# Moving the K, V and WO loads of a decode kernel from SyncE's hardware queue to GpSimd's software queue

## The chip, the cores and the metric

One core of one Trainium2 chip. The metric is the device time of one execution in microseconds (us). The 25 executions of the kernel before lie between 1273.79 and 1274.54 us. The word "tile" below means one load of K or of V: 128 partitions by 64 KiB, 8.39 MB.

## The reference, cut to what matters

A gated mix of two branches for two tokens. Branch A is one decode step of grouped attention with a cache of 32768 positions, 8 key-value heads, 2 batches; K and V caches together are 537 MB in bf16. Branch B is a small dense layer with a GELU.

```python
g = sigmoid((x * gate_w).sum(-1, keepdims=True))
q = x @ wq                                   # x: 2 x 448, wq: 448 x 4096
p = softmax(q . K * Dh**-0.5)                # K, V: 2 x 8 x 32768 x 256
a = (p . V) @ wo                             # wo: 4096 x 448
b = gelu(x @ w1 + b1) @ w2 + b2              # w1: 448 x 1792, w2: 1792 x 448
out = g * a + (1 - g) * b
```

## The kernel before

The kernel streams K and V through a ring of three slots, each of one tile. All large loads are issued by SyncE, in the order of one list:

```python
order = [("WQ", 0), ("W12", 0)]              # WQ and W12 (w1 and w2) share slot 0
for i in range(NTILES + LAG):                # NTILES = 32, LAG = 2
    if i < NTILES: order.append(("K", i))
    if i >= LAG and i - LAG < LASTV: order.append(("V", i - LAG))
order += [("V", LASTV), ("WO", 0)]
# K0 -> slot 1, K1 -> slot 2, K2 -> slot 0, V0 -> slot 1, K3 -> slot 2, V1 -> slot 0 ...

def released(d):                             # what must have been done before the slot may be refilled
    kind, idx = d
    return {"K": ("S", idx, NCK // 2 - 1), "V": ("PV", idx), "WQ": "QT", "W12": "FB"}[kind]

def prog_sp(E):
    for d in order:
        for pd in before_of[d]:
            E.wait("pe", released(pd))
        # ... e.dma_start(...) for WQ (2 loads), W12 (3), WO (4), the last V (3), every other K or V (1)
```

So K2 cannot be issued before FB, the last matmul that reads W12. TensorE (PE) and VectorE (DVE) work in a fixed order as well:

```python
# PE
do_QT()      # waits for WQ: the query
do_GG()
do_HT()      # waits for W12
do_FB()      # branch B; its end releases slot 0
# ... then scores S(0), S(1), ...; each waits for DVE's transposes of that K tile
# DVE
gelu1(); gelu2()                             # branch B, needs HT
for i in range(LAG): K(i)                    # 8 transposes of 2.27 us for each K tile, in the ring
# ...
```

ACT (ScalarE) issues six very small loads (x, the gate, the biases) on its own hardware queue during the first 3 us.

## Time and profile before

| | before |
|---|---|
| median of 2 runs | 1273.99 us |
| DMA read | 547.4 MB, 430 GB/s over the span |
| DVE busy, PE busy | 54%, 55% |

The page of the kernel before. The row DMA is the mean busy share of the 16 DMA engines in tenths, in 40 slices of the span; under it the GB/s of each slice; then the queue with packets, MB and share of the engines' time.

```profile
span 1272.2 us, 8282 instructions
...
DMA  9999999999999999999999999999999999999998
GB/s 409 429 433 429 437 441 427 433 427 441 431 437 435 429 431 433 439 431 437 435 429 431 439 433 431 439 433 429 431 441 431 435 437 431 431 433 439 431 423 353
...
q1 hardware_dynamic: 10804, 547.43, 99.6%
```

The DMA row shows what bounds the kernel: 9 tenths or more from the first slice to the last but one. DVE and PE are half idle. One data packet here is one row of one partition: 75 loads of 128 rows, and for each load 16 packets of 4 bytes, are 10800 of q1's 10804 packets. A packet of a K tile is therefore 64 KiB, one of WQ 24 KiB.

The start, in lines of the timeline of single engines (start, duration, engine, line of the kernel, operation, output and input, count, and in brackets the idle time before and its releaser; SPq is SyncE issuing a load):

```profile
0.74 0.88 SPq L370 DMA_DIRECT2D ring<-in_A_wq_dram  x2
...
3.54 28.30 SPq L391 DMA_DIRECT2D ring<-in_A_k_cache_dram  x3
...
9.60 0.61 DVE L677 TENSOR_TENSOR gp_sb<-pexp,PT 2x448 f32<-2x448 bf16 x1 [5.52 <-DMA PT<-in_gate_w_dram]
...
12.73 3.55 PE L419 MATMUL ps_s<-xT,ring 128*128 128x2 bf16 x128 [8.24 <-DMA ring<-in_A_wq_dram]
...
20.86 0.34 PE L438 MATMUL ps_m<-xT,ring 128*128 128x2 bf16 x3 [2.63 <-DMA ring<-in_B_w_dram]
...
40.20 17.66 DVE L720 STREAM_TRANSPOSE ring<-ring 128x2048 uint32<-128x2048 uint32 x8 [10.33 <-DMA ring<-in_A_k_cache_dram]
...
59.55 17.66 DVE L720 STREAM_TRANSPOSE ring<-ring 128x2048 uint32<-128x2048 uint32 x8 [1.70 <-DMA ring<-in_A_k_cache_dram]
```

In this trace the queue serves the loads first in, first out. WQ and W12 are used at 12.73 and 20.86 us, K0 is there for DVE at 40.20 and K1 at 59.55, which is 19.35 us later, the time of one tile. The first line of K stands for three issues; the third, K2, was made at 31.5 us, after FB, and lay in the queue for some 26 us: its first packet starts at 57.3. (That is from the packet records of the packed trace: start, length, size and queue of every packet.) The DMA never ran dry. The line of gp_sb: two tiny gate loads on ACT's queue, issued by 1.9 us, were waited for until 9.60.

The same by stretches (from and to, length, the engines' busy time and instructions, granted TensorE clock, DMA share, GB/s; PEld is TensorE's weight load). A packet is counted whole in the stretch in which it starts, so a share can pass 1:

```profile
core 0: us, PE busy (x) PEld busy (x) DVE busy (x) ACT busy (x) POOL busy (x), PEclk, DMA share, GB/s
0.00:180.00 180.00, 106.58 (x798) 30.98 (x518) 105.36 (x88) 9.58 (x36) 3.31 (x14) 0.90 1.00 428
180.00:1180.00 1000.00, 539.64 (x3358) 103.37 (x1306) 549.73 (x403) 32.37 (x143) 0.00 (x0) 0.77 1.00 434
58.00:70.00 12.00, 9.44 (x36) 1.90 (x19) 10.45 (x5) 0.00 (x0) 0.00 (x0) 0.86 1.02 438
130.00:134.00 4.00, 4.00 (x20) 0.86 (x9) 4.00 (x3) 0.00 (x0) 0.00 (x0) 1.00 0.98 426
```

### The profile page before, as it was taken

To read this page: it belongs to the slowest core of one execution; us is meant where nothing else is said; L and a number is where in the kernel's file an instruction comes from. 1 tells how busy PE (TensorE), PEld (TensorE's weight loads), DVE (VectorE), ACT (ScalarE), POOL (GpSimd) and SP (SyncE) were. 2 spreads that over 40 slices of the span, in tenths; PEclk is the share of its full clock that TensorE was granted. 3 is DMA by queue.
4 is the path that set the end of the run, shared out by engine and by line. 5 is a ranking of instruction groups with operands and counts; after the bars stand their busy time and mean duration, and the time that the engine had idled before them with its cause. 6 is when DMAs were issued, how large, how long until landed. Compare 5 with 4: busy or idle time off the path is not lost.

```text
span 1272.2 us, 8282 instructions
## 1 busy us (share of the span) xinstructions
PE 693.5 (55%) x4640; PEld 145.3 (11%) x2112; DVE 686.0 (54%) x529; ACT 43.8 (3%) x184; POOL 3.3 (0%) x14
## 2 busy tenths in 40 slices
PE   4566566545566444765445655445664546654465
PEld 3111111100111000111001111001110001110011
DVE  2675546745376553655635567353665536556351
ACT  1000000000000000000000000000000000000000
POOL 1000000000000000000000000000000000000000
PEclk9978887777887677877778877788877788867786
DMA  9999999999999999999999999999999999999998
GB/s 409 429 433 429 437 441 427 433 427 441 431 437 435 429 431 433 439 431 437 435 429 431 439 433 431 439 433 429 431 441 431 435 437 431 431 433 439 431 423 353
DMA packets 10973, 547.62 MB, mean 430 GB/s; under 512 B 1352, under 2 KB 1616, under 8 KB 1872
## 3 DMA queue, kind: packets, MB, share of 16 engines
q1 hardware_dynamic: 10804, 547.43, 99.6%
q8 instruction: 9, 0.15, 0.0%
q14 instruction: 4, 0.03, 0.0%
q10 hardware_dynamic: 156, 0.01, 0.0%
HBM read 547.43 MB, written 0.00 MB: 430 GB/s over the span
## 4 chain that ended last, share of the span: by engine, by line
DMA 63%; DVE 20%; PE 14%; issue 3%; SPq 0%; another core or an unknown queue 0%; DVEq 0%
DMA ring<-in_A_k_cache_dram 60%; DVE ring L720 18%; PE ps_s L487 4%; PE ps_s L334 4%; PE ps_o L334 3%; DMA ring<-in_A_v_cache_dram 3%; DVE mx L724 1%; PE ps_o L536 1%; PE ps_m L496 0%; PE ps_m L501 0%; DVE gmax L726 0%; PE ps_f L548 0%; DVE gmx L730 0%; SPq L376 0%
## 5 line engine op out<-in xcount | busy, mean ns | idle before, releaser
L720 DVE STREAM_TRANSPOSE ring<-ring 128x2048 uint32<-128x2048 uint32 x256 | 565.2, 2274 | 393.0 <-DMA ring<-in_A_k_cache_dram 392.8
L487 PE MATMUL ps_s<-ring,Abd 128*128 128x512 bf16 x1024 | 426.1, 416 | 429.8 <-DVE ring L720 429.4
L334 PE MATMUL ps_s<-ring,Abd 128*128 128x512 bf16 x1024 | 422.8, 413 | 0.0
L487 PEld LDWEIGHTS ps_s<-ring,Abd 128*128 128x128 bf16 x1024 | 106.0, 104 | 851.5 <-DVE ring L720 483.5
L334 PE MATMUL ps_o<-ring,PT 128*24 128x512 bf16 x1504 | 111.9, 404 | 0.0
L536 PE MATMUL ps_o<-ring,PT 128*24 128x512 bf16 x544 | 57.1, 418 | 12.8 <-DMA ring<-in_A_v_cache_dram 12.8
L506 PE MATMUL ps_f<-o_sb,selg 128*32 128x257 f32 x32 | 17.0, 636 | 83.4 <-DVE o_sb L761 83.4
L761 DVE SCALAR_TENSOR_TENSOR o_sb<-ps_o,mask,o_sb 128x256 f32<-128x256 f32 x112 | 54.2, 484 | 9.1 <-PE ps_o L536 5.1
L724 DVE TENSOR_REDUCE mx<-ps_s 128x1 f32<-128x1024 f32 x16 | 19.6, 1225 | 60.0 <-PE ps_s L334 60.0
L632 ACT ACTIVATE negm<-ps_m 128x1 f32<-128x1 f32 x16 | 2.7, 171 | 1157.6 <-PE ps_m L501 1157.6
L737 DVE STREAM_TRANSPOSE PT<-pexp 128x1024 bf16<-128x1024 bf16 x16 | 19.9, 1244 | 36.8 <-PE ps_o L334 36.8
L536 PEld LDWEIGHTS ps_o<-ring,PT 128*24 128x24 bf16 x544 | 14.6, 98 | 102.3 <-issue 85.3
L734 DVE COPY ls<-lsum 128x1 f32<-128x1 f32 x16 | 2.5, 154 | 31.8 <-ACT pexp L636 31.8
L626 ACT COPY Abd<-qrep 32x16 bf16 (+1 forms) x128 | 19.4, 199 | 0.6
L636 ACT ACTIVATE pexp<-ps_s,negm 128x1024 bf16<-128x1024 f32 x16 | 17.8, 1113 | 1.7
L496 PE MATMUL ps_m<-ident_f,mx 128*1 128x128 f32 x32 | 6.1, 270 | 21.1 <-DVE mx L724 21.1
L758 DVE TENSOR_SCALAR o_sb<-ps_o,mask 128x256 f32<-128x256 f32 x16 | 7.6, 475 | 15.7 <-PE ps_o L334 15.7
L506 PEld LDWEIGHTS ps_f<-o_sb,selg 128*32 128x32 f32 x32 | 2.9, 141 | 101.5 <-DVE o_sb L761 101.5
L501 PE MATMUL ps_m<-ones_f,gmx 1*128 1x1 f32 x32 | 6.0, 256 | 9.9 <-DVE gmx L730 9.9
L726 DVE TENSOR_REDUCE gmax<-ps_m 1x2 f32<-1x128 f32 x16 | 4.5, 278 | 7.5 <-PE ps_m L496 7.5
L419 PE MATMUL ps_s<-xT,ring 128*128 128x2 bf16 x128 | 3.6, 165 | 8.2 <-DMA ring<-in_A_wq_dram 8.2
L501 PEld LDWEIGHTS ps_m<-ones_f,gmx 1*128 1x128 f32 x32 | 4.7, 183 | 14.6 <-DVE gmx L730 14.6
(76 smaller groups left out, 61.5 us busy)
## 6 DMA issues: line engine op xcount, KB each, us to landing
ring<-in_A_v_cache_dram SPq DMA_DIRECT2D x1, 4096.0 KB, 26.8
ring<-in_A_v_cache_dram SPq DMA_DIRECT2D x2, 2048.0 KB, 33.5
ring<-in_A_wq_dram SPq DMA_DIRECT2D x1, 3072.0 KB, 10.6
ring<-in_B_w_dram SPq DMA_DIRECT2D x1, 1568.0 KB, 17.9
ring<-in_A_wo_dram SPq DMA_DIRECT2D x1, 1568.0 KB, 32.4
ring<-in_B_w_dram SPq DMA_DIRECT2D x1, 1344.0 KB, 13.7
ring<-in_A_wo_dram SPq DMA_DIRECT2D x1, 1344.0 KB, 35.3
ring<-in_A_wq_dram SPq DMA_DIRECT2D x1, 512.0 KB, 11.4
```

Of the source, the lines that this page charges most:

```text
L334: return e.add_instruction(mybir.InstMatmult(name=f"I-{nc.next_id()}", engine=mybir.EngineType.PE, ldweights=False, ins=[e.lower_ap(x), e. ...
L487: fn = lambda e, o=o, x=x, st=st, sp=sp, s=s, w=w: e.matmul(o, a_win(s, w), x, start=st, stop=sp, skip_group_check=True)
L501: E.ins(lambda e: e.matmul(ps_m[:, C_BC:C_BC + 1], gmx[:, :], ones_f[0:1, 0:1], start=True, stop=True), key=("M2", g))
L506: E.ins(lambda e: e.matmul(ps_oa, selg[:, :], o_sb[:, :], start=False, stop=False, skip_group_check=True), key=("OT", g))
L536: fn = lambda e, o=o, x=x, wt=wt, st=st, sp=sp, j=j: e.matmul(o, wt, x, start=st, stop=sp, skip_group_check=True)
L626: E.ins(lambda e, o=o, Q=Q, c=c: e.copy(o[:, :, c:c + 2], qrep[32 * Q:32 * Q + 32, :, bass.ds(E.dyn(2 * g, 2), 2)]), key=(("A", g) if (Q = ...
L636: E.ins(lambda e: e.activation(pexp[:, :].rearrange("p (r i a) -> p i r a", r=CR, i=2), ps_s[:, :].rearrange("p (i r a) -> p i r a", i=2, ...
L720: E.ins(lambda e: e.transpose(k_words(idx, blk), k_words(idx, blk)), key=("T", idx, blk))
L724: E.ins(lambda e: e.tensor_reduce(mx[:, :], ps_s[:, :], AX.X, ALU.max), key=("MX", g))
L737: E.ins(lambda e: e.transpose(PT[:, :], pexp[:, :]), key=("PT", g))
L758: E.ins(lambda e, p=p, m=m: e.tensor_scalar(o_sb[:, 0:Dh], p, m, None, op0=ALU.mult), key=("OS0", g))
L761: E.ins(lambda e, p=p, m=m: e.scalar_tensor_tensor(out=o_sb[:, 0:Dh], in0=p, scalar=m, in1=o_sb[:, 0:Dh], op0=ALU.mult, op1=ALU.add), key= ...
```

## The change

K, V and WO are issued by GpSimd; the profile shows them on a queue that it calls software_dynamic, and "software descriptors" below means this path. WQ and W12 stay with SyncE. GpSimd first does its setup (constants), then the loads, in the same relative order. The intent is a test of the other path: it frees SyncE, and nothing else.

```diff
-        def prog_sp(E):
+        def loads(E, kinds):
...
             for d in order:
+                if d[0] not in kinds:
+                    continue
                 for pd in before_of[d]:
                     E.wait("pe", released(pd))
...
+        def prog_pool(E):
+            # ... the setup of constants, as before
+            loads(E, ("K", "V", "WO"))
+
+        def prog_sp(E):
+            loads(E, ("WQ", "W12"))
             E.wait("dve", "mix")
```

(The rest gives WQ a semaphore of its own and swaps two lists of programs.)

More of the change, by code (lines that the diff above doesn't have):

```diff
@@ L196, in bass_gated_mix__gqa_block_cached__dense_activation_gelu__decode_kernel @@
         sch.stream(f"pW{i}", 16)
-    for nm in ("d_w12", "d_x", "d_gw", "d_b", "d_out"):
+    for nm in ("d_wq", "d_w12", "d_x", "d_gw", "d_b", "d_out"):
         sch.stream(nm, 16)
@@ L337, in keep_matmul @@
                 stop_tensor_calc=stop, tile_size=tile[0], tile_position=tile[1], bass_skip_group_check=True))
-        def prog_pool(E):
-            E.ins(lambda e: e.memset(ident_b[:], 0.0), key="ms0")
-            E.ins(lambda e: e.memset(ident_f[:], 0.0), key="ms1")
-            E.ins(lambda e: e.memset(ones_f[:], 1.0), key="ones")
-            E.ins(lambda e: e.memset(xm[:], 0.0), key="xm0")
-            E.wait("pool", "ms0")
-            E.ins(lambda e: e.affine_select(out=ident_b[:], in_=ident_b[:], compare_op=ALU.not_equal, fill=1.0,
-                                          base=0, pattern=[[-1, P]], channel_multiplier=1), key="idb")
-            E.wait("pool", "ms1")
-            E.ins(lambda e: e.affine_select(out=ident_f[:], in_=ident_f[:], compare_op=ALU.not_equal, fill=1.0,
-                                          base=0, pattern=[[-1, P]], channel_multiplier=1), key="idf")
-            E.ins(lambda e: e.memset(Abd[:], 0.0), key="A0")
-            E.ins(lambda e: e.memset(tsel[:], 0.0), key="t0")
-            E.wait("pool", "t0")
-            for b in range(Bn):
-                E.ins(lambda e, b=b: e.affine_select(
-                    out=tsel[:, 136 * b:136 * b + 136], in_=tsel[:, 136 * b:136 * b + 136], compare_op=ALU.not_equal,
-                    fill=1.0, base=256 - 128 * b, pattern=[[-1, 136]], channel_multiplier=-8), key=f"ts{b}")
-        def prog_sp(E):
+        def loads(E, kinds):
             def dma(fn, stream, key):
@@ L369, in prog_sp @@
                     for i, (o, src, _) in enumerate(parts):
-                        dma(lambda e, o=o, src=src: e.dma_start(o, src), "slot0", ("wq", i))
+                        dma(lambda e, o=o, src=src: e.dma_start(o, src), "d_wq", ("wq", i))
                 elif kind == "W12":
@@ L392, in prog_sp, with dma @@
                         f"slot{slot_of[d]}", ("fill", d))
+        def prog_pool(E):
+            E.ins(lambda e: e.memset(ident_b[:], 0.0), key="ms0")
+            E.ins(lambda e: e.memset(ident_f[:], 0.0), key="ms1")
+            E.ins(lambda e: e.memset(ones_f[:], 1.0), key="ones")
+            E.ins(lambda e: e.memset(xm[:], 0.0), key="xm0")
+            E.wait("pool", "ms0")
+            E.ins(lambda e: e.affine_select(out=ident_b[:], in_=ident_b[:], compare_op=ALU.not_equal, fill=1.0,
+                                          base=0, pattern=[[-1, P]], channel_multiplier=1), key="idb")
+            E.wait("pool", "ms1")
+            E.ins(lambda e: e.affine_select(out=ident_f[:], in_=ident_f[:], compare_op=ALU.not_equal, fill=1.0,
+                                          base=0, pattern=[[-1, P]], channel_multiplier=1), key="idf")
+            E.ins(lambda e: e.memset(Abd[:], 0.0), key="A0")
+            E.ins(lambda e: e.memset(tsel[:], 0.0), key="t0")
+            E.wait("pool", "t0")
+            for b in range(Bn):
+                E.ins(lambda e, b=b: e.affine_select(
+                    out=tsel[:, 136 * b:136 * b + 136], in_=tsel[:, 136 * b:136 * b + 136], compare_op=ALU.not_equal,
+                    fill=1.0, base=256 - 128 * b, pattern=[[-1, 136]], channel_multiplier=-8), key=f"ts{b}")
+            loads(E, ("K", "V", "WO"))
+        def prog_sp(E):
+            def dma(fn, stream, key):
+                E.ins(fn, key=key, stream=stream)
+            loads(E, ("WQ", "W12"))
             E.wait("dve", "mix")
@@ L409, in do_QT @@
                 E.wait("act", "xT")
-                E.wait("slot0", ("wq", 1))
+                E.wait("d_wq", ("wq", 1))
                 for h in range(Hq):
@@ L793, in prog_dve @@
                       key=("mix" if q == 1 else None))
-        progs = {"pool": prog_pool, "sp": prog_sp, "pe": prog_pe, "act": prog_act, "dve": prog_dve}
+        progs = {"sp": prog_sp, "pool": prog_pool, "pe": prog_pe, "act": prog_act, "dve": prog_dve}
         engs = {nm: _Eng(sch, nm) for nm in progs}
@@ L807, in run @@
                 progs[nm](engs[nm])
+            block.sync(lambda eng: run("sp", eng))
             block.gpsimd(lambda eng: run("pool", eng))
-            block.sync(lambda eng: run("sp", eng))
             block.tensor(lambda eng: run("pe", eng))
```

## The prediction

> **What bounds the kernel now.** The DMA engines. The page gives 547.42 MB read at a mean of 430 GB/s; the stretch from 100 to 1200 us shows DMA share 1.00 at 433 GB/s. DVE (54%) and PE (55%) wait; 60% of the chain of waits is K loads. A K or V tile is 8.39 MB, 19.4 us at 433 GB/s; V loads land 36.6 us after issue, so even then some 17 us of earlier work are queued. Only an idle gap of the DMA or a lower rate costs time.
>
> **What moves.** 70 loads go from SyncE's queue to GpSimd's; WQ and W12 stay. An issue costs SyncE 0.33 us. [...] With 17 us queued that is hidden. Bytes and rows (64 KiB per partition) stay, so I expect 431-434 GB/s again.
>
> **The step that costs: the start.** Before, one FIFO queue served WQ, W12, K0, K1: WQ was there at 12.7 us (first query matmul), W12 at 20.9, K0 at 40.2, K1 at 59.6, and K2, which waits until WQ and W12 are consumed, was issued at 31.9, long before the queue ran dry. After, K0 and K1 come on another queue from about 4 us (GpSimd's setup ends at 4.02). [...] two tiny gate loads on ACT's queue, issued by 1.9 us, were waited for until 9.6, about one 24 KiB WQ packet (0.9 us) for each of their small ones. A K packet is 64 KiB, 2.4 us. Working the turns through (estimate, 27 KB/us per engine): K0 lands at 29-30 us, WQ at 40-45, K1 at 51, W12 at 57.
>
> FB, the last reader of W12, came 10.3 us after W12: K2 is issued at about 68 and moves from 70: DMA idle from 57 to 70, 13 us. DVE transposes K0 only after the GELU (program order), from 66 to 84 instead of 40 to 58. The ring of three slots then starts with compute behind: V0 issued at 88, K3 at 106, V1 at 133 after K3 has landed at 129: 6 us more of idle DMA. By 160 us the queue is two deep again, but lost time is not won back. Sum: +19 us. The tail changes by 1-2 us at most.
>
> **Prediction.** 1293 us, 8 in 10 between 1279 and 1314. Chances: faster by over 2% 0.01, within 2% 0.70, slower 0.29.
>
> **What would show it.** Right: DMA share near zero at 57-70 us and a dip near 130; WQ consumed after 35 us, W12 after 50; DVE's first transpose of the ring at about 66; K2's issue at about 68; after 160 us 433 GB/s and DVE waiting for K loads as before. Wrong: WQ still at 13 us, or a lower rate between 200 and 1200 us.
>
> **What would make it wrong.** Software descriptors of another size, or a slow engine, that lower the steady rate: each 1% is 12 us. [...] Turns by bytes rather than packets: then WQ and W12 land earlier and the loss shrinks.

+19 us is 13 (57 to 70 us) and 6 (near 130). That the 17 us queued would hide whatever a software load adds was the author's estimate. The turns packet by packet were read from the gate loads of the trace before. In its packet records two packets of 896 bytes, the gate's by their place in the queue, start at 6.42 and 8.28 us, and packets of 4 bytes at 7.37 and 9.23: steps of 0.91 to 0.95 us, where one WQ row takes 0.91. The estimate's 27 KB/us per engine is 433 GB/s over 16 engines.

## The result, and the profile after

| | before | after |
|---|---|---|
| median | 1273.99 us (2 runs) | 1294.80 us (2 runs) |
| ratio, 95% interval | | 1.0163 [1.0138, 1.0187] |

A ratio, here and below, is the mean time of one kernel's fast runs over that of the other's of the same rounds, so not quite the ratio of the medians. The change costs 20.8 us. The page after:

```profile
span 1292.5 us, 8282 instructions
...
DMA  9789899999999999999999999999999999999998
GB/s 402 332 347 430 360 422 440 433 426 446 424 428 446 426 426 446 428 434 436 430 436 432 430 444 426 428 444 428 428 442 430 432 436 432 438 430 430 440 421 357
...
q0 software_dynamic: 9936, 540.55, 96.8%
q1 hardware_dynamic: 724, 6.88, 1.3%
```

The second, third and fifth slices of GB/s (332, 347, 360) are where this row differs; the rest looks as before. The stretches, with the columns of before, tell the same:

```profile
0.00:180.00 180.00, 86.36 (x698) 27.04 (x474) 90.40 (x82) 9.59 (x36) 8.21 (x23) 0.93 0.89 377
180.00:1180.00 1000.00, 546.05 (x3406) 104.48 (x1326) 547.45 (x402) 32.40 (x143) 27.43 (x52) 0.78 1.00 434
58.00:70.00 12.00, 8.75 (x134) 7.64 (x134) 3.31 (x10) 0.23 (x1) 0.00 (x0) 1.00 0.01 2
130.00:134.00 4.00, 3.85 (x19) 0.77 (x8) 1.47 (x2) 0.00 (x0) 0.00 (x0) 1.00 0.06 20
```

From 180 to 1180 us both kernels move 434 GB/s. In the first 180 us the changed one moves 377 GB/s instead of 428; 51 GB/s for 180 us are 9.2 MB, which take 21 us at 433 GB/s. That is the loss, within 0.4 us. Most of it lies in two stretches in which the DMA does next to nothing: 58 to 70 us and 130 to 134 us. (Cut finer, they reach from about 57.4 to 71.7 and from about 129 to 135.8. By the packet records, those of instructions left out, the 16 engines stood idle for a mean of 14.2 us between 57 and 72 us and of 5.0 us between 128 and 136.)

The start in the timeline, as shown for before (POOL is GpSimd):

```profile
0.74 0.87 SPq L353 DMA_DIRECT2D ring<-in_A_wq_dram  x2
...
4.09 1.20 POOL L374 DMA_DIRECT2D ring<-in_A_k_cache_dram  x2
...
41.72 3.55 PE L428 MATMUL ps_s<-xT,ring 128*128 128x2 bf16 x128 [37.20 <-DMA ring<-in_A_wq_dram]
...
59.39 0.34 PE L447 MATMUL ps_m<-xT,ring 128*128 128x2 bf16 x3 [12.17 <-DMA ring<-in_B_w_dram]
...
68.30 35.20 DVE L729 STREAM_TRANSPOSE ring<-ring 128x2048 uint32<-128x2048 uint32 x16
...
70.50 0.53 POOL L374 DMA_DIRECT2D ring<-in_A_k_cache_dram  x1 [65.20 <-PE ps_f L464]
...
133.09 17.66 DVE L729 STREAM_TRANSPOSE ring<-ring 128x2048 uint32<-128x2048 uint32 x8 [2.53 <-DMA ring<-in_A_k_cache_dram]
...
134.56 0.53 POOL L374 DMA_DIRECT2D ring<-in_A_v_cache_dram  x1 [26.54 <-PE ps_s L334]
```

K0 and K1 are issued at 4.09 us, only half a microsecond later than before, but WQ is used at 41.72 instead of 12.73 and W12 at 59.39 instead of 20.86. FB then releases slot 0, and K2 is issued at 70.50, when the queues have been empty for 13 us. DVE begins on K0 at 68.30 although K0 landed 27.2 us after its issue, at 31.3 (K1 landed 49.0 us after its own, at 53.7). From then on compute is behind: V1 waits for the scores of K2 and is issued at 134.56, when K3 has already landed (133.09), and the DMA idles a second time.

In steady state nothing changed: V loads land 36.4 us after issue (36.6 before), K loads 49.5 (49.7). A GpSimd issue took 0.53 us and a SyncE issue 0.33. GpSimd's issues took 527 to 530 ns for all V loads and 527 to 673 for all K loads, though some came while DVE transposed (those at 89.95 and 134.56 us).

### The profile page after: what moved, and what is told of

It reads as the page before. It is cut to its first block, busy times and chain, and to the rows that moved or that the text cites. A ratio compares the mean times of both kernels' runs of the same rounds, so it can differ in the third digit from the quotient of the medians.

```text
span 1292.5 us, 8282 instructions
## 1 busy us (share of the span) xinstructions
PE 691.9 (54%) x4640; PEld 145.0 (11%) x2112; DVE 685.7 (53%) x529; ACT 43.9 (3%) x184; POOL 40.4 (3%) x84
## 4 chain that ended last, share of the span: by engine, by line
DMA 58%; DVE 22%; PE 13%; issue 3%; another core or an unknown queue 3%; ACT 0%; POOL 0%; SPq 0%; DVEq 0%
DMA ring<-in_A_k_cache_dram 52%; DVE ring L729 20%; PE ps_s L496 3%; PE ps_o L334 3%; PE ps_s L334 3%; DMA ring<-in_A_wq_dram 3%; DMA ring<-in_A_v_cache_dram 3%; DVE mx L733 1%; PE ps_o L545 1%; PE ps_m L505 0%; PE ps_m L510 0%; DVE gmax L735 0%; PE ps_m L447 0%; PE ps_s L428 0%
## 5 line engine op out<-in xcount | busy, mean ns | idle before, releaser
L545 PE MATMUL ps_o<-ring,PT 128*24 128x512 bf16 x544 | 57.6, 423 | 12.7 <-DMA ring<-in_A_v_cache_dram 12.7
L374 POOL DMA_DIRECT2D ring<-in_A_v_cache_dram x31 | 16.4, 528 | 960.1 <-PE ps_s L334 957.1
L374 POOL DMA_DIRECT2D ring<-in_A_k_cache_dram x32 | 17.0, 532 | 211.8 <-PE ps_o L334 129.5
L743 DVE COPY ls<-lsum 128x1 f32<-128x1 f32 x16 | 2.5, 154 | 31.8 <-ACT pexp L645 31.8
```

What stands on the lines that cost most here:

```text
L374: dma(lambda e, src=src, d=d: e.dma_start(cut(slot_of[d], 0, SLOT), src), f"slot{slot_of[d]}", ("fill", d))
L545: fn = lambda e, o=o, x=x, wt=wt, st=st, sp=sp, j=j: e.matmul(o, wt, x, start=st, stop=sp, skip_group_check=True)
```

## The experiments

The theory: software descriptors cost nothing that shows; the loss is an accident of order at the start, because two queues with work at the same time take turns here, packet by packet, and the queue with 64 KiB packets gets most of the time (2.42 us for such a packet, 0.91 for a WQ row of 24 KiB). The rivals: software descriptors cost something on each load; turns waste DMA time in themselves; turns go by bytes.

| run | what differs | median us | ratio to before, 95% | WQ, W12 used at | GB/s of the first 180 us |
|---|---|---|---|---|---|
| before | | 1273.95 | | 12.7, 20.9 | 428 |
| after | | 1294.80 | 1.0163 [1.0138, 1.0187] | 41.7, 59.4 | 377 |
| e2 | no software: K0, K1 on ACT's queue | 1293.62 | 1.0154 [1.0137, 1.0170] | 24.7, 59.4 | 382 |
| e3 | one hardware queue, K0, K1 first | 1294.20 | 1.0158 [1.0141, 1.0175] | 50.9, 59.5 | 382 |
| e4 | after, K0 and K1 in 8 KiB rows | 1275.20 | 1.0009 [0.9992, 1.0026] | 16.0, 31.3 | 427 |
| e5 | all loads on GpSimd | 1274.89 | 1.0005 [0.9991, 1.0019] | 13.4, 21.7 | 427 |
| e1 | after, K0 waits for W12 | 1277.82 | 1.0028 [1.0015, 1.0042] | 12.3, 20.7 | 417 |
| e6 | after, only K1 waits for W12 | 1277.66 | 1.0027 [1.0014, 1.0041] | 31.8, 40.2 | 417 |
| e7 | K0, K1 on SyncE, rest on GpSimd | 1292.55 | 1.0144 [1.0127, 1.0161] | 12.4, 21.0 | 382 |
| e8 | e7, K2 waits for K1 | 1278.20 | 1.0034 [1.0018, 1.0051] | as e7 | 417 |

All outputs were correct. Beside e1, e5 and e6 the kernel before had a median of 1274.15 us, beside e8 1273.96. The difference lies in the first 180 us: from 180 to 1180 us every one of them moved 433 or 434 GB/s.

### e2: two hardware queues, no software

```diff
+            E.wait("pool", "ts1")            # GpSimd's setup done, as in the changed kernel
+            loads(E, K0 and K1)              # on ACT, behind its six small loads
...
-            loads(E, ("K", "V", "WO"))       # GpSimd
-            loads(E, ("WQ", "W12"))          # SyncE
+            loads(E, all the others)         # SyncE
```

> No software descriptors at all: K0 and K1 are issued at about 4 us on ACT's hardware queue, everything else on SyncE's. Theory (taking turns between any two queues): WQ used at 39-44 us, W12 at 57-60, K2 issued at 68-72, DMA idle for some 13 us before it and about 5 us near 130, 1290-1298 us. Rival (software descriptors are the cost): 1273-1277 us.

1293.62 us. The loss is there without one software descriptor. Timeline and stretches of this run:

```profile
4.05 0.85 ACTq L374 DMA_DIRECT2D ring<-in_A_k_cache_dram  x2
...
24.68 3.55 PE L429 MATMUL ps_s<-xT,ring 128*128 128x2 bf16 x128 [20.18 <-DMA ring<-in_A_wq_dram]
...
59.44 0.34 PE L448 MATMUL ps_m<-xT,ring 128*128 128x2 bf16 x3 [29.25 <-DMA ring<-in_B_w_dram]
...
70.09 0.33 SPq L374 DMA_DIRECT2D ring<-in_A_k_cache_dram  x1
```

```profile
58.00:70.00 12.00, 8.75 (x134) 7.63 (x134) 3.25 (x10) 0.23 (x1) 0.00 (x0) 1.00 0.01 3
130.00:134.00 4.00, 3.32 (x16) 0.77 (x8) 2.56 (x2) 0.00 (x0) 0.00 (x0) 1.00 0.02 4
```

W12, K2's issue and both idle stretches are where they were in the changed kernel. One number missed: WQ was used at 24.7 us, not at 39 to 44. On ACT's queue K0 stands behind the small loads, which were waited for until 12.6 us, so most of WQ had gone through before the first K packet. No run tests that reading by itself, but the bytes agree with it: in the first 10 us the DMA moved 3.19 MB, which WQ's first load (3.15 MB) almost fills, while by then in the changed kernel, by its packet records, 16 rows of K0 (1.05 MB) had started, the first at 7.9 us. It made no difference, since W12, which comes last, decides when K2 is issued.

### e3: one hardware queue, another order

```diff
-order = [("WQ", 0), ("W12", 0)]
+order = [("K", 0), ("K", 1), ("WQ", 0), ("W12", 0)]
...
-    if i < NTILES:
+    if 2 <= i < NTILES:
```

> One hardware queue again, but K0 and K1 are issued ahead of WQ and W12. Theory (what costs is only that W12 lands behind both K tiles): K0 lands at 21-24 us, K1 at 41-43, WQ at 50-53, W12 at 57-60, K2 issued at 68-72, the same two idle stretches of the DMA, 1290-1298 us. Rival (the taking of turns itself wastes DMA time): 1273-1280 us. It also shows how long a hardware load takes on an idle DMA (K2), to set against 23.5 us of the software one in the changed kernel.

1294.20 us, with no second queue for the large loads at all.

```profile
50.94 3.56 PE L419 MATMUL ps_s<-xT,ring 128*128 128x2 bf16 x128 [46.44 <-DMA ring<-in_A_wq_dram]
...
59.45 0.34 PE L438 MATMUL ps_m<-xT,ring 128*128 128x2 bf16 x3 [3.01 <-DMA ring<-in_B_w_dram]
...
70.09 0.33 SPq L391 DMA_DIRECT2D ring<-in_A_k_cache_dram  x1
```

W12 and K2 are where they were in e2, and the DMA moved 2 GB/s from 58 to 70 us and 4 from 130 to 134. So the loss is the same without turns among the large loads: it is enough that W12 lands behind both K tiles. From 20 to 56 us this run and the changed kernel both moved 411 GB/s. On an idle DMA, K2 landed 23.4 us after its issue here, 23.4 in e2 and 23.5 from software in the changed kernel.

### e4: the same two queues, smaller packets

```diff
-dma(lambda e: e.dma_start(cut(slot, 0, SLOT), src), ...)
+n = 8 if d in (("K", 0), ("K", 1)) else 1
+for i in range(n):
+    c0, c1 = i * SLOT // n, (i + 1) * SLOT // n
+    dma(lambda e: e.dma_start(cut(slot, c0, c1 - c0), src[:, c0:c1]), ...)
```

> The changed kernel, with K0 and K1 each cut into 8 loads of 8 KiB rows instead of one of 64 KiB rows; all else equal. Theory (turns packet by packet, so small K packets give way to WQ and W12): WQ used at 14-18 us, W12 at 29-32, K2 issued at 39-43, no idle DMA, 1273-1278 us. Rival (turns by bytes, or K given precedence by its queue): WQ used near 40 us, W12 near 58, 1292-1297 us.

1275.20 us. The bytes, the queues, the issuing engine and the time of the first K issue are those of the changed kernel. Only K0's and K1's rows are 8 KiB long instead of 64, and each of the two tiles comes in 8 loads.

```profile
4.10 8.50 POOL L377 DMA_DIRECT2D ring<-in_A_k_cache_dram  x16
...
15.98 3.55 PE L431 MATMUL ps_s<-xT,ring 128*128 128x2 bf16 x128 [11.46 <-DMA ring<-in_A_wq_dram]
...
31.25 0.34 PE L450 MATMUL ps_m<-xT,ring 128*128 128x2 bf16 x3 [9.77 <-DMA ring<-in_B_w_dram]
...
42.36 0.53 POOL L377 DMA_DIRECT2D ring<-in_A_k_cache_dram  x1 [29.76 <-PE ps_f L467]
```

The 16 issues took GpSimd 8.5 us; the changed kernel has 2 for these tiles. Still WQ came 26 us sooner and W12 28 us sooner, and K2 was issued at 42.36, before the two K tiles had gone through. Turns by bytes would not depend on the length of K's rows.

This run leaves one rival, for it cut the loads as well as the rows: the queues might take turns by whole loads. The changed kernel itself settles that. WQ's first load, all in 24 KiB rows, took about twice as long to land there as before (lines of the two pages, before and after; KB, us to landing):

```profile
ring<-in_A_wq_dram SPq DMA_DIRECT2D x1, 3072.0 KB, 10.6
ring<-in_A_wq_dram SPq DMA_DIRECT2D x1, 3072.0 KB, 20.2
```

It was issued 3.3 us ahead of K0, so with turns by loads nothing of K would have come between its rows. In the packet records the two alternate row by row: K0's rows start, in groups of 16 (as many as there are DMA engines), at about 8.1, 11.4 and 14.8 us and WQ's at 7.2, 10.6 and 13.9, a period of 3.3 us, which is one row of WQ (0.91 us) and one of K0 (2.42 us).

### e5 and e1: one order again, with software descriptors

e5 has GpSimd issue WQ and W12 too, ahead of its setup. e1 is the changed kernel with one wait.

```diff
 def prog_pool(E):                            # e5
+    loads(E, ("WQ", "W12"))
     # ... setup
     loads(E, ("K", "V", "WO"))
...
+    E.wait_total("d_w12")                    # e1, ahead of GpSimd's loads of K, V and WO
```

> All loads on GpSimd's one software queue in the old order, WQ and W12 issued before GpSimd's own setup. Theory (software descriptors are free here, the loss was order): WQ used at 12-14 us, W12 at 20-22, K0 landed at 40-42, no idle stretch, 1274-1277 us. Rival (software descriptors add a cost somewhere): still above 1285 us.

> The changed kernel, with GpSimd waiting for W12 to land (about 20.5 us) before its first K load. Theory: order restored at the price of one gap of 1.5-3 us in the DMA while the first software load starts; no later idle stretch; 1275-1278 us. Rival (software descriptors): above 1285 us.

e5: 1274.89 us against 1274.15, and the interval of the ratio reaches from 0.9991 to 1.0019. Every large load is made by software there. So software descriptors cost this kernel at most 0.2%.

e1: 1277.82 us. Order is restored, for one gap: from 18 to 24 us the DMA moved 221 GB/s, which at 433 is 2.9 us of nothing, with W12 used at 20.69 us, K0 issued at 20.95 and 0 GB/s from 20 to 22. Over the first 180 us the deficit against before (417 to 428 GB/s) is 4.6 us, a little more than the 1.5 to 3 that I had expected.

### e6: half a dose

```diff
+                if d == ("K", 1):
+                    E.wait_total("d_w12")
```

> Half a dose: K0 is still issued at 4 us and takes turns with WQ and W12, K1 waits for W12 to land. Theory: WQ used at 29-33 us, W12 at 37-40, K2 issued at 48-51 while K1 is still moving (to about 60), so apart from one handover gap of 1.5-3 us no idle DMA: 1275-1279 us although W12 is 17 us late. A reading in which the loss grows with how late W12 is (17 of 37 us, so about half of 20) says 1283-1286 us.

1277.66 us.

```profile
31.82 3.55 PE L430 MATMUL ps_s<-xT,ring 128*128 128x2 bf16 x128 [27.31 <-DMA ring<-in_A_wq_dram]
...
40.19 0.34 PE L449 MATMUL ps_m<-xT,ring 128*128 128x2 bf16 x3 [2.87 <-DMA ring<-in_B_w_dram]
...
40.45 0.53 POOL L376 DMA_DIRECT2D ring<-in_A_k_cache_dram  x1 [35.68 <-DMA ring<-in_B_w_dram]
...
51.32 0.53 POOL L376 DMA_DIRECT2D ring<-in_A_k_cache_dram  x1 [10.34 <-PE ps_f L466]
```

W12 is used at 40.19 us, 19 us later than before, and the run costs no more than e1, which has its W12 on time. K2 is issued at 51.32, while K1 is still moving. The late W12 was free here, as K2 entered a queue that had not yet run dry; the loss is not proportional to the delay.

### e7: a run that missed, and e8

I meant e7 to give the start of before with software in the steady state: K0 and K1 return to SyncE, behind W12, the rest stays on GpSimd.

```diff
-            loads(E, ("K", "V", "WO"))           # GpSimd
-            loads(E, ("WQ", "W12"))              # SyncE
+EARLY = (("WQ", 0), ("W12", 0), ("K", 0), ("K", 1))
+            loads(E, lambda d: d not in EARLY)   # GpSimd
+            loads(E, lambda d: d in EARLY)       # SyncE
```

> K0 and K1 go back to SyncE's queue, behind WQ and W12; the other 68 K, V and WO loads stay on GpSimd. Theory (the whole loss is the start, where two queues take turns): the start is as before, WQ used at 12-13 us, W12 at 20-21, no idle DMA near 60 us, 1273-1276 us, V loads landing 36-37 us after issue. Rival (software descriptors cost something at each of the loads): 1285-1296 us, since 68 of 70 loads are still made by software.

1292.55 us: by what was expected, the rival had won. The timeline says otherwise:

```profile
32.17 0.68 POOL L377 DMA_DIRECT2D ring<-in_A_k_cache_dram  x1 [28.12 <-PE ps_f L469]
...
45.15 17.66 DVE L734 STREAM_TRANSPOSE ring<-ring 128x2048 uint32<-128x2048 uint32 x8 [15.17 <-DMA ring<-in_A_k_cache_dram]
...
66.83 0.54 POOL L377 DMA_DIRECT2D ring<-in_A_v_cache_dram  x1 [33.99 <-PE ps_s L337]
...
84.17 17.67 DVE L734 STREAM_TRANSPOSE ring<-ring 128x2048 uint32<-128x2048 uint32 x8 [21.36 <-DMA ring<-in_A_k_cache_dram]
...
105.83 0.53 POOL L377 DMA_DIRECT2D ring<-in_A_k_cache_dram  x1 [38.47 <-PE ps_s L337]
```

```profile
96.00:106.00 10.00, 8.56 (x38) 1.73 (x18) 6.27 (x4) 0.00 (x0) 0.17 (x1) 1.00 0.00 0
126.00:134.00 8.00, 7.25 (x55) 1.35 (x20) 8.00 (x5) 0.00 (x0) 0.53 (x1) 1.00 0.01 2
```

WQ and W12 were on time and K2 was issued at 32.17 us. But K2 was now alone on GpSimd's queue, and took turns with K0 and K1 on SyncE's. K0 came at 45.15 instead of 40.20, K1 at 84.17 instead of 59.55, behind K2, which landed 43.3 us after its issue, at 75.5. While these three moved, only V0 could be issued; K3 waits for the scores of K1 and came at 105.83, with the DMA empty from 96. The stretch from 126 to 134 us is empty too. It is the same accident one step later in the stream. e8 tests this reading with one more wait:

```diff
+                if d == ("K", 2):
+                    E.wait("d_k1", ("fill", ("K", 1)))
```

> The kernel of the run that missed (K0 and K1 on SyncE behind W12, the rest on GpSimd), with one wait added: GpSimd issues K2 only when K1 has landed (about 60 us). Theory (there K2 took turns with K0 and K1 on the other queue, so K1 landed at 84 instead of 60 us and both V0 and K3 came too late): K0 lands at 40-41, K1 at 59-60, one handover gap of 1.5-3 us, no other idle DMA, 1276-1279 us. Rival (handing the stream from a hardware to a software queue costs by itself, or software descriptors do): still 1285 us or more.

1278.20 us. K0 and K1 are back at 40.07 and 59.41 us, and what remains is one handover gap, as in e1 (8 GB/s from 58 to 60 us). 68 of the 70 loads are made by software in both; 14 us went away with the turns.

No experiment beats the kernel before. As long as the DMA moves 434 GB/s at most, which no run here exceeded from 180 to 1180 us, none could by much: it runs at that rate from its first packets to its last, so what is left is some 2 us before the first bytes (1.8 in its packet records) and 4 us after the last (WO's end at 1268.1 of 1272.2).

## Why the prediction was right

The prediction said 1293 us, and 1294.8 were measured.

- **The bound.** Right. The loss equals the bytes not moved in the first 180 us.
- **Software descriptors hidden in steady state.** Right: 434 GB/s in both, landing times within 0.2 us, and e5 at 1.0005. The predicted rate of 431 to 434 held.
- **Turns packet by packet at the start.** Right, and shown by e4, where only the rows and loads of K0 and K1 were cut and the loss went, together with the packet records, which show turns of one row. e2 shows that it is not a matter of software, e3 that the late W12 alone makes the loss. The estimate gave K0 29 to 30, WQ 40 to 45, K1 51, W12 57 us; the trace has K0 at 31.3, WQ used at 41.7, K1 at 53.7 and W12 used at 59.4.
- **K2 late, idle DMA.** Right, both stretches: 13 us predicted from 57 to 70, 14.2 of mean idle measured (W12 was used some 2 us after its estimated landing, and K2 issued at 70.50 instead of 68); 6 us predicted near 130, 5.0 measured. The two misses nearly cancel: the sum is 19.2 where 19 was predicted. That the number came so close is in part luck. The other 1.6 us of the 20.8 were not traced to a step.
- **DVE's transposes from 66 us, recovery by 160 us.** 68.30 us; and from 180 us on the rates are equal.
- **Not foreseen.** The biases on ACT's queue, behind K's packets too, were waited for until 41.0 us (12.8 before). This was harmless, as W12 was later still. And I missed, when designing e7, that the same turns would be taken between K1 and K2.

## What to carry to other kernels

A queue was also an order here. When the loads with 64 KiB rows moved to a second queue, they overtook the loads with smaller rows that were to go ahead of them (W12 used at 59.4 us instead of 20.9), by packets and not by bytes (31.3 us with 8 KiB rows, e4). Look for the load whose lateness delays a slot's release, and check whether the DMA has other work queued until then. If it had, the delay was free (e6: W12 19 us late, 1277.66 us against 1277.82 of e1); if not, the DMA idled for 14.2 and 5.0 us, and this kernel, bound by it, did not get the time back: 434 GB/s from 180 to 1180 us, before and after. Three ways out were measured: the loads that must land in order on one queue (e5, 1.0005), the overtaking loads' rows small (e4, 1.0009), or a wait between the queues, which cost 3.5 to 4.2 us (e1, e6, e8).
